# Logits maximum one step later with blanks in the work list; the opening's loads set by hand between the first transposing DMAs

## The chip, the core and the metric

The kernel runs on one core of a Trainium2 chip. The core has TensorE (PE: matrix products, written to PSUM), VectorE (DVE), ScalarE (ACT), GpSimd (POOL) and SyncE (SP), which here only issues DMAs; 16 DMA engines move the data. Each engine runs its own instructions in order and waits on semaphores for others. The metric is the device time of one execution in microseconds, lower is better.

## The reference

Attention over 8 batches of 8 heads, 576 positions, 64 wide, with a mask by blocks of 64; then a soft mixture of experts on the 4608 tokens of width 512 (8 experts with 4 slots each, so 32 slots), then a two-layer network. Cut to what matters:

```python
scores = scale * np.matmul(q, k.transpose(0, 1, 3, 2))
scores = np.where(mask, scores, -1000000000.0)        # mask: block_i >= block_j
scores = scores - np.max(scores, axis=-1, keepdims=True)
attn = np.exp(scores)
attn = attn / (np.sum(attn, axis=-1, keepdims=True) + 1e-09)
x = np.matmul(attn, v)                    # -> tokens x of shape (4608, 512)
logits = x @ phi                          # (4608, 32)
d = np.exp(logits - logits.max(0, keepdims=True))
d /= d.sum(0, keepdims=True) + 1e-09
slot_input = d.T @ x                      # per expert: relu(slot_input @ w1) @ w2
...
c = softmax over the slots;  y = c @ slot_out
h = np.maximum(y @ w_in, 0.0);  out = h * h @ w_out
```

## The kernel before, in words

The attention goes through 32 *pairs*: pair n is heads 2j and 2j+1 of batch n // 4, j = n % 4. `pair(n)` emits, in eight slots, the work of several pairs at once: the scores of pair n (`scores`, matmuls L572, L581, L590; ScalarE's exponentials `p` L610, and `pd` L592 for the last diagonal blocks; GpSimd's sums `ss` L615), the products with the values of pair n-1 (`pv`, L646 `xm`, L657 `tl`, L666 `sm`), the row maxima of pair n+2 (`maxpass`, matmuls L494, L502, L530; VectorE's `pm` and `ptl` L508, and L543 to L552 at its end, which write them into `qb`), and the splitting of pair n+3 into a high and a low half-precision part (`split`: ScalarE L451, VectorE L457; the key tile `ka` is then turned by a transposing DMA L464 into `s`, the high query is turned on TensorE L473).

Ahead of a split stands `scale`: ScalarE squares the keys and the queries (L389, tile `junk`, the sums in `ssq`), TensorE adds them over the partitions (L396, `ps_ssq`), and VectorE makes the factors (L401 to L421). `turn_qb(n)` turns the low query of pair n, with the maxima in it, by a transposing DMA into `t` (L483); it needs L552 of that pair. `s2copy` copies half of `s` from SBUF to SBUF (L980).

Around the pairs runs other work, popped from lists slot by slot: `aux` (the steps of `scale`; `None` is an empty slot), `dq` (SyncE's loads, two a slot: keys and queries of a batch L365 and L371 as well as L343 and L350, values L319 and L324, `phi` L332, weights), and `work`, the list that `batch(b)` makes for the soft mixture of the batch before: `logits(u)` for five blocks of tokens (GpSimd ends them, L762, in `lg` and `ltl`), `maxes` (VectorE L812, L813, and the copy `mx` L815: the maximum of the logits over the tokens of a batch), `running` (the maximum so far, L820), `weights` (the exponentials `d`, L831 to L840), `total` (L880), `tokens(u)` (TensorE L857 turns the attention's output, VectorE L867 multiplies it by the reciprocal of the softmax's sums into `x`), and `gather(u)` (TensorE L906 and L912, VectorE L919: `acc`). A batch's list is put in at the second pair of the next batch, and slots 1, 3, 4, 6 and 7 pop one item each, so five a pair.

The order of each engine's instructions is worked out by a scheduler from the program's order, estimated durations and dependences, except where `tc.manual_schedule(engines=...)` keeps the program's order for the engines it names. Before the change the opening (pairs 0 to 2 scaled, split and maximised ahead of the pair loop) keeps it for ScalarE alone; the pair loop keeps it for TensorE and SyncE. `order(x, y)` makes x come after y.

Of the kernel before, what the change touches and what calls it, by code (L numbers as in the profile page):

```python
# [13 lines left out]
ALU = mybir.AluOpType  # L14
AX = mybir.AxisListType
# [8 lines left out]
def tile_attn_soft_moe_ffn(  # L24
# [225 lines left out]
    def attention():  # L250
# [481 lines left out]
        def batch(b):  # L732
# [77 lines left out]
            def maxes():  # L810
                mxb = sm_p.tile([128, NSL], F32, tag="mxb", name="mxb")
                nc.vector.tensor_reduce(out=mxb, in_=lm.rearrange("p u s -> p s u"), axis=AX.X, op=ALU.max)  # L812
                nc.vector.tensor_tensor(out=mxb[0:64], in0=mxb[0:64], in1=ltl, op=ALU.max)  # L813
                mx4 = sm_p.tile([128, 4, NSL], F32, tag="mx4", name="mx4", bufs=1)
                nc.vector.tensor_copy(mx4, mxb.unsqueeze(1).to_broadcast([128, 4, NSL]))  # L815
                box["mx4"] = mx4
# [33 lines left out]
            def tokens(u, j0=0, j1=NJ):  # L850
# [9 lines left out]
                if j0 == NJ - 1:  # L860
# [5 lines left out]
                    return  # L866
                nc.vector.tensor_tensor(  # L867
                    out=box[u][0:w].rearrange("p (hp j d) -> p j hp d", hp=2, j=NJ)[:, j0:j1],
# [57 lines left out]
            if b == B - 1:  # L926
# [10 lines left out]
                [lambda u=u: logits(u) for u in range(5)]  # L937
                + [lambda: tokens(0), maxes, lambda: tokens(1), running, lambda: tokens(2), weights, lambda: tokens(3)]
                + [total, lambda: [gather(u) for u in range(4)], lambda: tokens(4), lambda: gather(4)]
            )  # L940
# [35 lines left out]
        def loads(k):  # L976
            for _ in range(min(k, len(dq))):
                dq.pop(0)()
# [3 lines left out]
        prepare()  # L982
        with tc.manual_schedule(engines={mybir.EngineType.Activation}):
            c0, c1, c2 = [scale([i]) for i in range(3)]
            for f in c0[:2] + c1[:1] + c0[2:]:
                f()
            sp0 = split(0)
            for f in (sp0[2], sp0[0], c1[1], c1[2], sp0[1], sp0[3]):
                f()
            sp1 = split(1)  # L990
            for f in (sp1[2], sp1[0], c2[0], c2[1], sp1[1], sp1[3], c2[2]):
                f()
            sp2 = split(2)
            sp2[2]()
            s2copy(0)
            m0 = maxpass(0)
            for f in m0[6:] + m0[:6] + [sp2[0], sp2[1], sp2[3]]:
                f()
        dq += load_v(0) + load_batch(1)[0] + load_batch(1)[1] + load_v(1) + [lambda hp=hp: load_phi(hp) for hp in range(2)]
        s3 = scale([AHEAD])  # L1000
        m1 = maxpass(1)
        for i, f in enumerate(m1[6:] + m1[:6]):
            if i >= 6 and s3:
                [g() for g in s3]
                s3 = []
            f()
            loads(1)
        for f in s3:
# [13 lines left out]
        def pair(n):  # L1022
# [43 lines left out]
            if n >= 7:  # L1066
                if ew:
                    dq.append(ew.pop(0))
                if len(decq) <= 6 and nraw[0] < NRAW:
                    nraw[0] += 1  # L1070
                    decq.append(nraw[0] - 1)
            if n == 1:
                aux += scale([4]) + scale([5])
            if n == 2:
                aux += scale([6])
            if n % 2 and n > 1:
# [28 lines left out]
            for i in range(8):  # L1105
                loads(2)
                for f in slot.get(i, []):
                    f()
                f = aux.pop(0) if aux else None
                if f:  # L1110
                    f()
                elif decq and i % 8:
                    dec_step()
                for _ in range((i in (1, 3, 4, 6, 7)) if n < N - 3 else 1 if n < N - 1 else 2):
                    if work:
                        work.pop(0)()
            if n == N - AHEAD - 1:
# [645 lines left out]
```

## Time and profile before

| | us |
|---|---|
| median of three runs | 875.07 |
| lowest and highest run | 869.28 and 875.86 |
| the profiled execution | 874.78 |
| its span, first to last instruction | 873.0 |
| TensorE busy in it | 816.3 (94%) |
| VectorE, ScalarE, GpSimd busy | 669.5, 627.8, 242.6 |

The profile is of one execution. It has a page (busy times, the span in 40 slices, the chain of waits that ended last, groups of instructions), and the trace behind it can be asked for timelines, lists of waits, and windows. A time in a timeline is counted from the span's start. "Wait" is the idle time of an engine ahead of an instruction, put down to what ended it.

### The profile page before, as it was taken

What the parts mean: (1) busy time and instruction counts of PE and PEld (TensorE: products, weight loads), DVE (VectorE), ACT (ScalarE), POOL (GpSimd) and SP (SyncE); (2) the same over time, 40 slices, a digit from 0 to 9 for tenths busy, and PEclk for the clock granted to TensorE, in tenths of its full rate; (3) what the DMA queues carried; (4) which work ended last, traced back from release to release, by engine and by line L of the source; (5) the groups of instructions that cost most, each with busy time, mean ns of one, the idle gap of its engine ahead of it and who ended that gap; (6) DMA issues with size and microseconds to landing.
All of it is one profiled execution on the core that took longest, in us unless ns stands there. A gap on an engine that the chain in (4) does not pass through costs nothing.

```text
span 873.0 us, 21653 instructions
## 1 busy us (share of the span) xinstructions
PE 816.3 (94%) x8741; PEld 598.9 (69%) x8741; DVE 669.5 (77%) x1546; ACT 627.8 (72%) x996; POOL 242.6 (28%) x394
## 2 busy tenths in 40 slices
PE   2779999899999999999995999999999999999997
PEld 1446767576666667676431554888888888888887
DVE  5857789989998987764724899787888888888880
ACT  5579787777878687744214889888888888888770
POOL 0245747556575757464000000000000000000000
PEclk9899999999999999999999899999999999999999
DMA  8798998999899978689999300101000000000002
GB/s 166 148 188 159 156 200 155 219 172 221 156 210 181 171 149 171 119 232 314 351 386 385 123 1 0 50 26 45 30 25 26 25 26 25 26 25 26 26 25 49
DMA packets 220356, 113.14 MB, mean 130 GB/s; under 512 B 192096, under 2 KB 194144, under 8 KB 220256
## 3 DMA queue, kind: packets, MB, share of 16 engines
q1 hardware_dynamic: 217600, 111.11, 55.1%
q8 instruction: 68, 1.11, 0.6%
q10 hardware_dynamic: 2656, 0.66, 0.4%
q14 instruction: 32, 0.26, 0.1%
HBM read 78.71 MB, written 9.44 MB: 101 GB/s over the span
## 4 chain that ended last, share of the span: by engine, by line
PE 71%; DMA 9%; DVE 6%; POOL 5%; ACT 4%; issue 2%; SPq 1%; ACTq 0%; POOLq 0%
PE ps_y L1575 14%; PE ps_z L1575 10%; PE ps_x L1575 10%; PE xm L646 7%; PE ps_sc L572 6%; DMA t<-qb 4%; PE ps_hb L1539 3%; DMA wch<-in_moe_w_dram 3%; POOL ul L762 2%; PE ps_max L494 2%; PE sm L666 2%; POOL ss L615 2%; PE po L1597 2%; PE ps_u L753 2%; PE tl L657 2%
## 5 line engine op out<-in xcount | busy, mean ns | idle before, releaser
L1575 PEld LDWEIGHTS <-ah 128*128 128x128 f16 x1792 | 174.8, 98 | 21.9 <-issue 0.8
L610 ACT ACTIVATE p<-ps_sc,es 128x512 f32<-128x512 f32 x192 | 130.1, 686 | 64.7 <-PE ps_sc L572 32.5
L1507 DVE TENSOR_TENSOR al<-a,ah 128x1024 f16<-128x1024 f32 (+1 forms) x128 | 138.5, 1124 | 16.9 <-ACT ah L1562 15.5
L508 DVE TENSOR_REDUCE pm<-ps_max 128x4 f32<-128x512 f32 x160 | 106.1, 681 | 39.5 <-PE ps_max L502 39.3
L615 POOL TENSOR_TENSOR ss<-p 128x384 f32<-128x384 f32 (+1 forms) x128 | 86.3, 693 | 156.3 <-ACT p L610 156.1
L1562 ACT CAST ah<-a 128x1024 f16<-128x1024 f32 (+1 forms) x128 | 114.4, 936 | 15.0 <-DVE a L1507 13.4
L572 PE MATMUL ps_sc<-t,s 128*128 128x512 f16 (+3 forms) x512 | 108.4, 305 | 12.7 <-DMA t<-qb 7.6
L1668 POOL TENSOR_TENSOR ot<-u,p 128x256 f32<-128x256 f32 x16 | 12.5, 781 | 374.2 <-DVE u L1639 358.5
L1575 PE MATMUL ps_y<-bh,al 128*128 128x256 f16 x384 | 104.6, 273 | 0.0
L1575 PE MATMUL ps_y<-bl,ah 128*128 128x256 f16 x384 | 104.6, 272 | 0.0
L1575 PE MATMUL ps_y<-bh,ah 128*128 128x256 f16 x384 | 104.6, 272 | 0.0
L615 POOL TENSOR_TENSOR ss<-ss,p 128x320 f32<-128x320 f32 (+1 forms) x128 | 98.3, 768 | 18.7 <-ACT p L610 11.1
L1575 PEld LDWEIGHTS <-al 128*128 128x128 f16 x896 | 87.6, 98 | 10.2
L1401 ACT ACTIVATE r<-ps_hb,cts_h 128x1024 f32<-128x1024 f32 x64 | 71.2, 1112 | 30.0 <-PE ps_hb L1539 29.4
L646 PE MATMUL xm<-p,ar_hi 128*64 128x256 f32 (+3 forms) x512 | 87.2, 440 | 0.0
L1507 DVE TENSOR_TENSOR a<-a 128x256 f32<-128x256 f32 x192 | 76.1, 424 | 3.9
L1575 PE MATMUL ps_x<-bh,ah 128*128 128x256 f16 x256 | 69.8, 273 | 0.0
L1575 PE MATMUL ps_z<-bh,ah 128*128 128x256 f16 x256 | 69.8, 273 | 0.0
L1575 PE MATMUL ps_x<-bl,ah 128*128 128x256 f16 x256 | 69.8, 273 | 0.0
L1575 PE MATMUL ps_z<-bh,al 128*128 128x256 f16 x256 | 69.8, 273 | 0.0
L1575 PE MATMUL ps_x<-bh,al 128*128 128x256 f16 x256 | 69.8, 273 | 0.0
L1575 PE MATMUL ps_z<-bl,ah 128*128 128x256 f16 x256 | 69.8, 273 | 0.0
(272 smaller groups left out, 1777.9 us busy)
## 6 DMA issues: line engine op xcount, KB each, us to landing
wch<-in_moe_w_dram SPq DMA_DIRECT2D x18, 1024.0 KB, 12.8
ar_hi<-in_v_dram SPq DMA_DIRECT2D x64, 128.0 KB, 3.9
raw<-in_moe_w_in_dram SPq DMA_DIRECT2D x16, 512.0 KB, 5.7
out_dram<-ot SPq DMA_DIRECT2D x32, 256.0 KB, 2.1
ar_hi<-in_moe_w_dram SPq DMA_DIRECT2D x6, 1024.0 KB, 8.3
s<-s SPq DMA_DIRECT2D x32, 144.0 KB, 3.7
ar_hi<-in_k_dram SPq DMA_DIRECT2D x16, 256.0 KB, 4.5
ar_hi<-in_q_dram SPq DMA_DIRECT2D x16, 256.0 KB, 4.7
```

The source lines that it names most:

```text
L494: nc.tensor.matmul(ps[:, c0:c0 + 128 * (u + 1)].rearrange("p (s c) -> p s c", c=128), t1[:, 2 * u + hp, :], s1[:, hp:2 * u + 2:2, :], star ...
L508: nc.vector.tensor_reduce(out=o, in_=i, axis=AX.X, op=ALU.max)
L572: nc.tensor.matmul(ps[:, c0:c0 + w].rearrange("p (s c) -> p s c", c=128), kk[:, 2 * t + hp, :], qq[:, 2 * u0 + hp:8:2, :], start=(c0 == 0 ...
L610: exps[:] = [nc.scalar.activation(out=pt, in_=ps, func=AF.Exp, scale=es[:, 0:1])]
L615: add = lambda o, x, y: nc.gpsimd.tensor_tensor(out=o, in0=x, in1=y, op=ALU.add)
L646: nc.tensor.matmul(box["xm"][64 * hp:64 * hp + 64, 128 * t:512], vs[:, t, hp, :], r, start=(t == 0), stop=(t == 3),)
L657: nc.tensor.matmul(box["tl"][64 * hp:64 * hp + 64, 0:64], vs[:, t, hp, :] if t < NU else v_tail(b)[:, j, :], r, start=(t == 0), stop=(t == ...
L1401: nc.scalar.activation(out=r[:, c0:c1], in_=ps[:, c0:c1], func=AF.Relu, **kw)
L1507: sub = lambda o, a, b: nc.vector.tensor_tensor(out=o, in0=a, in1=b, op=ALU.subtract)
L1539: nc.tensor.matmul(ps[:, 512 * j + 256 * a:512 * j + 256 * a + 256], w[:, 128 * f:128 * f + 128], c, start=True, stop=True,)
L1562: nc.scalar.copy(v(hl[n % 2][0][:, 2 * kq:2 * kq + 2], s), v(a7[n, kq], s))
L1575: nc.tensor.matmul(acc[:, 0:HM], a[:, k], b[:, k], start=bool(first and k + j == 0), stop=(k == KH - 1 and j == 2), skip_group_check=not f ...
```

## The change

Three edits. In `batch(b)` the list gets the order `tokens(0), tokens(1), maxes, tokens(2), running, tokens(3), None, weights, None, total, gathers, tokens(4), gather(4)`, so `maxes` comes one item later, there are two empty items, and all from `running` on come one to three items later; the reduction of `maxes` is tied behind the last token multiply on VectorE, but in the last batch. In the opening SyncE's order is the program's too, `dq` begins with the keys and queries of batch 1 and has the values of batch 0 behind them, and `loads` is called between the splits. And `scale` for pairs 4, 5 and 6 is put in one pair earlier each (pairs 0, 1 and 2; in pair 0 behind four empty slots), each alone and with an empty slot between squares and factors.

```diff
--- before.py
+++ after.py
@@ -809,7 +809,9 @@
 
             def maxes():
                 mxb = sm_p.tile([128, NSL], F32, tag="mxb", name="mxb")
-                nc.vector.tensor_reduce(out=mxb, in_=lm.rearrange("p u s -> p s u"), axis=AX.X, op=ALU.max)
+                x = nc.vector.tensor_reduce(out=mxb, in_=lm.rearrange("p u s -> p s u"), axis=AX.X, op=ALU.max)
+                if b < B - 1:
+                    order(x, box["x"])
                 nc.vector.tensor_tensor(out=mxb[0:64], in0=mxb[0:64], in1=ltl, op=ALU.max)
                 mx4 = sm_p.tile([128, 4, NSL], F32, tag="mx4", name="mx4", bufs=1)
                 nc.vector.tensor_copy(mx4, mxb.unsqueeze(1).to_broadcast([128, 4, NSL]))
@@ -864,7 +866,7 @@
                             func=AF.Copy, scale=rc[0:w, u, 2 * j0 + hp:2 * j0 + hp + 1],
                         )
                     return
-                nc.vector.tensor_tensor(
+                box["x"] = nc.vector.tensor_tensor(
                     out=box[u][0:w].rearrange("p (hp j d) -> p j hp d", hp=2, j=NJ)[:, j0:j1],
                     in0=pt[0:w, 0:128 * nj].rearrange("p (j hp d) -> p j hp d", hp=2, j=nj),
                     in1=rc[0:w, u, 2 * j0:2 * j1].rearrange("p (j hp) -> p j hp", hp=2).unsqueeze(3).to_broadcast(
@@ -935,8 +937,9 @@
                 )
             return (
                 [lambda u=u: logits(u) for u in range(5)]
-                + [lambda: tokens(0), maxes, lambda: tokens(1), running, lambda: tokens(2), weights, lambda: tokens(3)]
-                + [total, lambda: [gather(u) for u in range(4)], lambda: tokens(4), lambda: gather(4)]
+                + [lambda: tokens(0), lambda: tokens(1), maxes, lambda: tokens(2), running]
+                + [lambda: tokens(3), None, weights, None, total]
+                + [lambda: [gather(u) for u in range(4)], lambda: tokens(4), lambda: gather(4)]
             )
 
         def recycle():
@@ -980,31 +983,42 @@
         s2copy = lambda n: nc.sync.dma_start(out=s2[n % NB2][0:64], in_=T[n][1][0:64])
         loads(len(dq))
         prepare()
-        with tc.manual_schedule(engines={mybir.EngineType.Activation}):
+        dq += load_batch(1)[0] + load_batch(1)[1] + load_v(0) + load_v(1) + [lambda hp=hp: load_phi(hp) for hp in range(2)]
+        s3 = scale([AHEAD])
+        E = mybir.EngineType
+
+        def opening():
             c0, c1, c2 = [scale([i]) for i in range(3)]
             for f in c0[:2] + c1[:1] + c0[2:]:
                 f()
             sp0 = split(0)
             for f in (sp0[2], sp0[0], c1[1], c1[2], sp0[1], sp0[3]):
                 f()
+            loads(3)
             sp1 = split(1)
             for f in (sp1[2], sp1[0], c2[0], c2[1], sp1[1], sp1[3], c2[2]):
                 f()
+            s2copy(0)
+            loads(2)
             sp2 = split(2)
             sp2[2]()
-            s2copy(0)
+            loads(3)
             m0 = maxpass(0)
             for f in m0[6:] + m0[:6] + [sp2[0], sp2[1], sp2[3]]:
                 f()
-        dq += load_v(0) + load_batch(1)[0] + load_batch(1)[1] + load_v(1) + [lambda hp=hp: load_phi(hp) for hp in range(2)]
-        s3 = scale([AHEAD])
-        m1 = maxpass(1)
-        for i, f in enumerate(m1[6:] + m1[:6]):
-            if i >= 6 and s3:
-                [g() for g in s3]
-                s3 = []
-            f()
-            loads(1)
+
+        with tc.manual_schedule(engines={E.SP}):
+            with tc.manual_schedule(engines={E.Activation, E.SP}):
+                opening()
+            m1 = maxpass(1)
+            for i, f in enumerate(m1[6:] + m1[:6]):
+                if i >= 6 and s3:
+                    [g() for g in s3]
+                    s3 = []
+                if i in (2, 5):
+                    loads(1)
+                f()
+            loads(2)
         for f in s3:
             f()
         work, aux, decq, nraw = [], [], [], [0, 0]
@@ -1069,10 +1083,8 @@
                 if len(decq) <= 6 and nraw[0] < NRAW:
                     nraw[0] += 1
                     decq.append(nraw[0] - 1)
-            if n == 1:
-                aux += scale([4]) + scale([5])
-            if n == 2:
-                aux += scale([6])
+            if n < 3:
+                aux += [None] * (0 if n else 4) + scale([n + 4], 1)
             if n % 2 and n > 1:
                 ns = [i for i in (n + AHEAD + 1, n + AHEAD + 2) if i < N]
                 aux += scale(ns, 2) if ns else []
@@ -1112,8 +1124,9 @@
                 elif decq and i % 8:
                     dec_step()
                 for _ in range((i in (1, 3, 4, 6, 7)) if n < N - 3 else 1 if n < N - 1 else 2):
-                    if work:
-                        work.pop(0)()
+                    f = work.pop(0) if work else None
+                    if f:
+                        f()
             if n == N - AHEAD - 1:
                 dq += wchunks(2)
             if n == N - 1:
```

The code lines behind L812 move by 2 and behind L983 by 3 and more, so that `x` is L869, the copy `mx` L817 and `s2copy` L983 in the changed kernel. The numbers behind a tile's name count tiles and differ for the same tile.

SyncE in the opening, before, from the first turned key tile (`s_248`, pair 0) to the fourth (`s_476`, pair 3); `t_381` and `t_467` are the turned queries of pairs 0 and 1:

```order
L371 DMA ar_hi<-in_k_dram 64x4x64
L980 DMA s_0_144<-s_248 64x1152
L371 DMA ar_hi<-in_k_dram 64x4x64
L464 DMA_TRANSPOSE s_293<-ka 128x9x128
L365 DMA ar_hi<-in_k_dram 128x8x64
L980 DMA s_1_145<-s_293 64x1152
L365 DMA ar_hi<-in_k_dram 128x8x64
L464 DMA_TRANSPOSE s_339<-ka 128x9x128
L365 DMA ar_hi<-in_k_dram 128x8x64
L483 DMA_TRANSPOSE t_381<-qb_141 128x9x128
L483 DMA_TRANSPOSE t_467<-qb_142 128x9x128
L464 DMA_TRANSPOSE s_476<-ka 128x9x128
```

The same place after (`s_299` is the key tile of pair 1, `s_485` of pair 3, `t_392` and `t_473` the queries):

```order
L365 DMA ar_hi<-in_k_dram 128x8x64 x2
L983 DMA s_1_145<-s_299 64x1152
L464 DMA_TRANSPOSE s_348<-ka 128x9x128
L365 DMA ar_hi<-in_k_dram 128x8x64
L371 DMA ar_hi<-in_q_dram 64x4x64 x2
L319 DMA ar_hi<-in_v_dram 128x4x64
L483 DMA_TRANSPOSE t_392<-qb_141 128x9x128
L365 DMA ar_hi<-in_q_dram 128x8x64 x2
L483 DMA_TRANSPOSE t_473<-qb_142 128x9x128
L365 DMA ar_hi<-in_q_dram 128x8x64 x2
L324 DMA ar_hi<-in_v_dram 64x4x64
L464 DMA_TRANSPOSE s_485<-ka 128x9x128
```

The keys' loads of batch 1 stand ahead of the queries' transposes, its queries' loads around them, and the loads of the values (L319, L324), which were ahead of the first key transpose, stand behind.

TensorE at the end of the scores of pair 0 (L590), before:

```order
L590 LDWEIGHTS s_248
L590 MATMUL ps_sc<-t_247,s_248 128x128
L590 LDWEIGHTS s_0_144
L590 MATMUL ps_sc<-t_381,s_0_144 128x128
L572 LDWEIGHTS s_293
L572 MATMUL ps_sc<-t_292,s_293 128x512
```

And after:

```order
L590 LDWEIGHTS s_251
L590 MATMUL ps_sc<-t_250,s_251 128x128
L590 LDWEIGHTS s_0_144
L590 MATMUL ps_sc<-t_392,s_0_144 128x128
L396 MATMUL ps_ssq<-ssq,ones 128x2
L572 LDWEIGHTS s_299
L572 MATMUL ps_sc<-t_298,s_299 128x512
```

The norm of pair 4 (L396), which before stood in the middle of pair 1 behind the second part of its maxima, now stands ahead of the first score of pair 1.

ScalarE there, before, from the exponentials of pair 0 on:

```order
L610 ACTIVATE p<-ps_sc,es 128x512 x5
L592 ACTIVATE pd<-ps_sc,es 128x128
L610 ACTIVATE p<-ps_sc,es 128x512
L389 ACTIVATE junk,ssq<-ar_hi 128x576
L695 COPY xt<-xm 128x512
L698 COPY xt<-tl 128x64
L610 ACTIVATE p<-ps_sc,es 128x512 x2
L389 ACTIVATE junk,ssq<-ar_hi 128x576
```

And after:

```order
L610 ACTIVATE p<-ps_sc,es 128x512 x4
L389 ACTIVATE junk,ssq<-ar_hi 128x576
L610 ACTIVATE p<-ps_sc,es 128x512
L592 ACTIVATE pd<-ps_sc,es 128x128
L389 ACTIVATE junk,ssq<-ar_hi 128x576
L610 ACTIVATE p<-ps_sc,es 128x512
L389 ACTIVATE junk,ssq<-ar_hi 128x576
L451 ACTIVATE qa<-ar_hi,sig 128x576
```

The squares of pair 4 (the first two of L389) stand ahead of the first exponential of pair 1; those of pair 5 begin behind it.

VectorE in the second pair that holds the list of batch 0, around `maxes`, after (before, L812 stood ahead of the first `x` of the list, in the row ahead of L421):

```order
L869 TENSOR_TENSOR x<-ps_x,rc 128x4x2x64
L508 TENSOR_REDUCE pm_146<-ps_max 128x4
L508 TENSOR_REDUCE pm_146<-ps_max 128x2x2
L869 TENSOR_TENSOR x<-ps_x,rc 128x4x2x64
L508 TENSOR_REDUCE pm_146<-ps_max 128x4
L812 TENSOR_REDUCE mxb<-lg 128x32
L508 TENSOR_REDUCE pm_146<-ps_max 128x4
L815 TENSOR_TENSOR mxb<-mxb,ltl 64x32
L869 TENSOR_TENSOR x<-ps_x,rc 128x4x2x64
L817 COPY mx_1855<-mxb 128x128
L543 TENSOR_REDUCE ps_max<-pm_146 128x2x2
L457 SCALAR_TENSOR_TENSOR qb_142<-ar_lo,sig,qa 128x9x64
```

The reduction, the maximum with the tail and the copy stand behind the second and third `x` now.

VectorE in the first pair of the batch after, up to the L552 that releases a turned query, after (before, the multiply of 64 partitions stood behind the L552 of the pair ahead, and an `acc` in this stretch ahead of the reciprocals):

```order
L719 RECIPROCAL rc<-ps_sT 128x2x8 x2
L723 RECIPROCAL rc<-ps_sT 64x8
L869 TENSOR_TENSOR x<-ps_x,rc 64x4x2x64
L508 TENSOR_REDUCE pm_146<-ps_max 128x4
L196 SCALAR_TENSOR_TENSOR tin<-dec_sq,raw 128x512
L921 SCALAR_TENSOR_TENSOR acc<-acc,al,ps_dx 128x512
L508 TENSOR_REDUCE pm_146<-ps_max 128x4
L202 TENSOR_SCALAR dec_sq<-tin 128x512
L543 TENSOR_REDUCE ps_max<-pm_146 128x2x2
L208 SCALAR_TENSOR_TENSOR dec_sq<-tin,dec_sq 128x512
L544 TENSOR_REDUCE ps_max<-pm_146 128x2x2
L457 SCALAR_TENSOR_TENSOR ka<-ar_hi,sig,ka 128x9x64
```

The multiply of the fifth block of tokens (`x`, 64 partitions) and an `acc` of a gather stand in this stretch, ahead of its L552, which is four rows on.

## Rows read from the trace of the kernel before

**Rows 1.** Head of the page; granted clock of TensorE in 40 slices.

```profile
span 873.0 us, 21653 instructions
...
PEclk9899999999999999999999899999999999999999
```

**Rows 2.** TensorE's timeline, opening: start, duration, line, operation; [idle before, what ended it].

```profile
32.94 0.58 PE L572 MATMUL ps_sc<-t,s 128*128 128x512 f16 x1 [2.93 <-DMA t<-qb]
...
40.65 0.28 PE L590 MATMUL ps_sc<-t,s 128*128 128x128 f16 x2
...
48.30 0.38 PE L396 MATMUL ps_ssq<-ssq,ones 128*128 128x2 f32 x2 [1.25 <-ACT junk L389]
...
49.93 0.38 PE L572 MATMUL ps_sc<-t,s 128*128 128x256 f16 x2
...
53.15 0.38 PE L396 MATMUL ps_ssq<-ssq,ones 128*128 128x2 f32 x2 [2.36 <-ACT junk L389]
...
61.56 0.39 PE L494 MATMUL ps_max<-s,t 128*128 128x128 f16 x2 [2.01 <-DMA s<-ka]
...
63.06 0.53 PE L396 MATMUL ps_ssq<-ssq,ones 128*128 128x2 f32 x2
...
66.15 0.40 PE L572 MATMUL ps_sc<-t,s 128*128 128x256 f16 x1
```

**Rows 3.** TensorE's waits, 100 to 420 us: total, times, longest.

```profile
PE ps_sc L572 <- DVE pm L508: 4.8, 4, 1.8
PE ps_sc L572 <- DMA t<-qb: 4.7, 5, 1.9
```

**Rows 4.** Windows of the opening: length, TensorE busy, granted clock, DMA share, GB/s.

```profile
33.00:39.00 6.00, 6.00 (x46) 0.50 0.57 109
53.00:55.00 2.00, 1.85 (x26) 1.00 1.10 241
63.00:66.00 3.00, 3.00 (x16) 0.50 1.15 219
```

**Rows 5.** SyncE's timeline (SPq: DMA issues; duration is that of issuing).

```profile
39.11 3.23 SPq L365 DMA_DIRECT2D ar_hi<-in_q_dram  x4
...
188.35 1.31 SPq L483 DMA_TRANSPOSE t<-qb  x1
...
237.07 1.31 SPq L483 DMA_TRANSPOSE t<-qb  x1
```

**Rows 6.** TensorE's timeline, start of a pair in the loop.

```profile
221.32 0.38 PE L572 MATMUL ps_sc<-t,s 128*128 128x512 f16 x1 [0.62 <-DMA t<-qb]
```

**Rows 7.** Windows of the loop, all engines' busy time, clock, DMA share, GB/s.

```profile
196.00:231.00 35.00, 32.39 (x465) 21.27 (x463) 32.01 (x86) 27.45 (x54) 20.16 (x32) 1.00 1.18 224
231.00:237.00 6.00, 6.00 (x104) 4.03 (x104) 6.00 (x13) 5.10 (x12) 3.18 (x5) 1.00 0.20 57
```

**Rows 8.** ScalarE's timeline, opening.

```profile
39.13 2.16 ACT L610 ACTIVATE p<-ps_sc,es 128x512 f32<-128x512 f32 x3 [0.70 <-PE ps_sc L572]
41.19 0.36 ACT L592 ACTIVATE pd<-ps_sc,es 128x128 f32<-128x128 f32 x1
...
47.48 0.67 ACT L389 ACTIVATE junk<-ar_hi 128x576 fp8e4<-128x576 f32 x1
```

**Rows 9.** Chain of waits, opening: start, duration up to the landing.

```profile
29.70 3.19 DMA t<-qb
...
56.86 4.65 DMA s<-ka
```

**Rows 10.** TensorE's waits, 285 to 420 us, the longest two.

```profile
PE ps_sc L572 <- DVE pm L508: 1.8, 1, 1.8
PE ps_dx L912 <- DVE x L867: 0.8, 1, 0.8
```

**Rows 11.** Instructions of L867 and L815: count, shortest/median/longest ns, when, shapes.

```profile
L867 DVE TENSOR_TENSOR x<-ps_x,rc x41: 273/673/692, 107.0 to 415.3; 128x512 f32<-128x512 f32 x28, 64x512 f32<-64x512 f32 x7, 128x256 f32<-128x256 f32 x3, 128x128 f32<-128x128 f32 x3
...
L815 DVE COPY mx<-mxb x8: 208/226/1349, 105.6 to 418.0; 128x128 f32<-128x128 f32 x8
```

## The prediction

> **What bounds the kernel now.** I read the head of the page first [rows 1]: the span is 873.0 us, and the profiled execution took 874.78 us, so 1.8 us lie outside the span; the median of the three runs is 875.07 us. TensorE's granted clock is below nine tenths in two slices of forty only, so what can be won is idle TensorE and a few stretches at the half clock. Next the timeline of TensorE in the opening [rows 2], for rows that end with a wait: 1.25 us at 48.30 and 2.36 us at 53.15 for ScalarE's squares (`junk`), ahead of the norms of pairs 4 and 5; 2.93 us at 32.94 for the first turned query tile, and 2.01 us at 61.56 for the turned key tile `s` of pair 4. Then the list of what TensorE waits for from 100 to 420 us [rows 3]: four waits for VectorE's `pm` reductions, 4.8 us together, and five for turned query tiles, 4.7 us.
>
> The clock is the third view [rows 4]. After the 2.93 us wait TensorE runs at 1.2 GHz from 33 to 39 us; after the 2.01 us wait it does so from 63 to 66 us. After the wait at 53.15 the clock stays at 2.4 GHz. The second dip has a price in the timeline [rows 2]: from the norm matmul to the 128x256 score of the same pair takes 48.30 to 49.93 = 1.63 us in pair 1 and 63.06 to 66.15 = 3.09 us in pair 2, so 1.46 us.
>
> Last, the loop. SyncE sits idle until VectorE ends the maximum of a pair (L552) and then issues a turned tile; this "restart" comes at 188.35 and at 237.07 [rows 5]. TensorE gets the first turned query tile of the next batch at 221.32, 32.97 us behind the restart [rows 6], and the DMA engines are queued more than full in that stretch (1.18), but at 0.20 in the 6 us before a restart [rows 7]. From 221.32 to the next restart TensorE's pace rules: 15.75 us. So a cycle of four pairs is a DMA part and a TensorE part. What is saved ahead of the transfer's landing inside the DMA part is given back as a longer wait for that transfer.
>
> **The opening.** The change takes the squares of pair 4 into pair 0, those of pair 5 into pair 1, and loads batch 1's keys and queries between the first transposing DMAs, when SyncE was idle.
> Removed: the waits at 48.30 and 53.15, 1.25 + 2.36 = 3.61 us, since both norms no longer stand behind those squares.
> Added: on TensorE the norm of pair 4 now stands between the last score of pair 0 (L590, ends at 40.65 + 0.28 = 40.93) and the first of pair 1, and in ScalarE's order the second square comes behind four exponentials, the first square, the fifth exponential and `pd`. From ScalarE's timeline [rows 8]: exponentials step by 2.16/3 = 0.69, so the fourth ends at about 40.5. The first square takes 0.67, the fifth exponential 0.69, `pd` 0.36 (each overlaps its neighbour by up to 0.1), and from a square's start to its norm matmul it is 48.30 − 47.48 = 0.82. So 40.5 + 0.67 + 0.69 + 0.36 + 0.82 = 43.0, less 0.2 for the overlaps, and TensorE waits 42.8 − 40.9 = 1.9 us where it did not. Bounds: 1.2 if the first square fits into ScalarE's idle time of 0.70 ahead of the row, 2.6 if a square waits for its load by one more square. I take 1.9. Behind that waiting instruction stand the score of pair 1 and all of `pv(0)`; nobody else waits for them, since ScalarE has the squares to do.
> The `s` of pair 4: SyncE issues it at 56.86 right behind a row of loads without a gap, and it lands 4.65 us later [rows 9]. After the change five loads fewer lie between the fourth key transpose and this one; a row of four loads takes 3.23 us on SyncE [rows 5], 0.8 each, and I take 0.65 for five of which two are short: 3.2 us. So it is issued at 53.6 and lands at 56.8 to 58.3 (3.19 us on idle queues, 4.65 on full ones). TensorE comes there at 59.55 − 3.61 + 1.9 = 57.8. So 0 to 0.5 of the 2.01 us stays; I take 0.5, as the queues are full. Then the half-clock stretch behind it goes as well: −1.46.
> At nothing: the values of batch 0's first pair are loaded later, now around the query transposes (29.70 on, [rows 9]) and behind the fourth key transpose; `pv(0)` reads them behind 43 us, and the wait for the square covers it. Without that cover it would wait for one load's landing at most, 3 to 5 us. The other moved loads stand ahead of where they were.
> One more term has only bounds. Loads of a key, of two query tails and of values, 0.5 MB, now stand right ahead of the first query transpose at 29.70, for which TensorE waits 2.93 us. It landed in 3.19 us on idle queues; the key transpose on full ones took 4.65 [rows 9]. So 0 to +1.46. At 241 GB/s [rows 4] 0.5 MB is 2.1 us, and SyncE was idle ahead of 29.70, so they have gone through by then: I take 0, nearest to the idle row. The Trainium skill speaks against that choice: DMA: Bandwidth & Descriptors, Latency and other measured facts, says that the fixed cost of a transfer grows with the load on HBM. The 3.19 against 4.65 here agrees. By the rule the first transpose would land later by part of the 1.46, and the sum would be up to 871.8.
> Opening: −3.61 + 1.9 − 1.5 − 1.46 = −4.7 us.
>
> **The loop.** `maxes` stands behind the second `tokens` step now, so GpSimd has one step more to finish the logits. VectorE's waits for it at L812 go, and with them those of TensorE for `pm`, which comes behind L812 on VectorE: 4.8 us. Three of the four lie in the DMA parts of cycles and come back as waits for `t<-qb`: gain 0. From 285 us on there is one of 1.8 us, and the next longest of all is for another thing [rows 10]: no turned tile is late there, so this one is won: −1.8.
> Against it: the work list is longer by two blanks, so `tokens(4)` lands in the next batch's first pair, whose `pm` pass ends in the L552 that restarts SyncE. VectorE is without a gap in 231 to 237 (6.00 of 6.00 us, [rows 7]), so the 0.67 us of L867 [rows 11] move the restart by that much. It counts in the three cycles that DMA limits: +2.0. In the pair of the fourth restart TensorE does not wait.
> `running`, `weights`, `total` and the gathers come one or two slots later; they write only what the next batch reads, so nothing waits within a pair; at the end of attention the weights' transfers, which follow TensorE, carry a shift through. I cost these at 0, ±0.3.
> Loop: −1.8 + 2.0 = +0.2.
>
> **Sum.** 874.78 − 4.7 + 0.2 = 870.3 by the profiled execution; by the median 0.3 more. I say 870.
>
> **The rivals.**
> (a) The loop does not give back. For it: every cycle also has TensorE's part, and SyncE waits for TensorE and VectorE inside the DMA part too, so an earlier TensorE may bring later issues forward. Against it: the 32.97 us and the queue at 1.18. Then all 4.8 us are won and the 2.0 are not lost: 874.78 − 4.7 − 4.8 = 865.3; faster by over 1%.
> (b) Slower: the four first pairs pay. The copy of the maxima (L815) took 1.349 us in its longest case against a median of 0.226 [rows 11], while GpSimd was at work on the sums. If the token multiply in its new place were stretched so, each of four restarts slips by 0.67 + 1.12 = 1.8 us, 7.2 together, and the 1.8 at `pm` is not won: 874.78 − 4.7 + 7.2 = 877.3. It decides from 1.2 us a restart on (4.7/4). Against it: the multiply has run beside GpSimd 41 times between 0.273 and 0.692 us, never longer [rows 11]. By the Trainium skill (SBUF — State Buffer, Who interferes with whom) a VectorE instruction with one input from SBUF, as this one (the other is in PSUM), does not contend with GpSimd, and a copy may; the rows agree for both. By it this rival is left with 0.67 a restart, 2.7 in all, and is not slower.
> (c) The new wait of 1.9 us at 41 brings a half-clock stretch of its own, as 2.01 did at 61.56, while 1.25 and 2.36 did not. Price 1.46 (or 3.0, half of 33 to 39): 871.8 to 873.3.
> (d) The opening does not do what it says, since the first query transpose or `s` of pair 4 is late by as much as it won: +1.46 + 1.5 + 1.46 on my sum: 874.7.
>
> **How the numbers follow.** Forecast (870) 0.43; (a) 0.19; (c) 0.20; (d) 0.12; (b) 0.06. About 1% (8.75 us) is what a measurement of this kernel can tell from no change: the three runs alone lie between 869.28 and 875.86. From 870 down to (a), with half a microsecond for its terms, 864.5; up past (d), 876. That leaves out most of (b) and the far side of (a). Faster by over 1% (below 866.3): (a) and a little of the forecast, 0.20. Slower by over 1% (above 883.8): only (b) with more than it is priced at, 0.02. Within: 0.78. The forecast's own range is 868.5 to 872.
>
> **What would show it.** In the changed profile: no wait at the norms of pair 1, a wait of 1.2 to 2.6 us for `junk` near 41 us; the `s` of pair 4 issued near 53.6 and a wait of at most 0.5 behind it; full clock from 60 to 68 us; no wait of VectorE at L812; in the loop the waits for `pm` gone but those for `t<-qb` longer by the same; restarts 0.7 us later behind the first scores of a batch. Wrong would be: waits for `t<-qb` that stay as short as they are (then a), the clock at half near 43 (c), a landing of the first query transpose past 33.5 (d).

## The result, and the profile after

The changed kernel takes 884.23 us (883.76 to 886.77), the kernel before 873.15 us in the runs beside it: a ratio of 1.0149, 95% interval 1.0116 to 1.0181. It is slower by 13.0 us at the middle of that interval, where 870 was forecast. The profiled execution took 884.6 us with a span of 882.8, so 9.8 us more than the profile before. One run of the old list below, which took 947.23 us at a mean granted clock of 0.846, is left out of its time and ratio.

The head of the page of the changed kernel, with the granted clock in 40 slices and the engines' shares of the chain that ended last, and those shares before:

```profile
span 882.8 us, 21649 instructions
...
PEclk9899999999999999999998899999999999999999
...
PE 68%; DVE 15%; DMA 8%; ACT 4%; issue 3%; SPq 1%; ACTq 0%; DVEq 0%
```

```profile
PE 71%; DMA 9%; DVE 6%; POOL 5%; ACT 4%; issue 2%; SPq 1%; ACTq 0%; POOLq 0%
```

VectorE's share of the chain is 15% in place of 6%. To find where that comes from, I cut the program in two at the last score of pair 3 (L590), which is ahead of all list work. TensorE's timeline there, first before, then after:

```profile
75.79 0.28 PE L590 MATMUL ps_sc<-t,s 128*128 128x128 f16 x2
```

```profile
70.12 0.28 PE L590 MATMUL ps_sc<-t,s 128*128 128x128 f16 x2
```

So the opening gives 5.7 us, and the rest of the program loses 9.8 + 5.7 = 15.5. A second cut, at the transpose of the last batch's maxima (L820 at 418.41 before, L822 at 427.05 after), splits that. Windows between the two cuts, before and then after (length, TensorE busy, granted clock, DMA share, GB/s):

```profile
75.79:418.41 342.62, 330.07 (x4573) 1.00 0.94 188
70.12:427.05 356.93, 333.35 (x4573) 0.99 0.93 182
```

So 14.3 of the 15.5 us are lost between the cuts: TensorE is idle for 23.6 us in place of 12.6, and busy for 3.3 us more. The other 1.2 us come behind the second cut and were not traced. TensorE's timeline of the changed kernel's opening, which answers to [rows 2]:

```profile
33.25 0.59 PE L572 MATMUL ps_sc<-t,s 128*128 128x512 f16 x1 [3.66 <-DMA t<-qb]
...
42.58 0.38 PE L396 MATMUL ps_ssq<-ssq,ones 128*128 128x2 f32 x2 [1.89 <-ACT junk L389]
```

The waits at 48.30, 53.15 and 61.56 are gone. One of 1.89 us has come at the norm of pair 4, and the wait for the first query transpose is 0.73 us longer. The loop is another picture. The whole list of what TensorE waits for from 100 to 420 us, which answers to [rows 3]:

```profile
PE ps_mx L822 <- DVE mx L817: 9.5, 6, 1.7
PE ps_ds L882 <- ACT d L842: 7.7, 7, 1.7
PE ps_dx L914 <- DVE x L869: 4.0, 7, 0.8
PE ps_sc L572 <- DMA t<-qb: 0.9, 1, 0.9
PE ps_x L859 <- ACT p L610: 0.5, 1, 0.5
```

That is 22.6 us. Before, the list came to 12.2: the 9.5 in [rows 3] and four small waits (1.1 for `p` at the norms, 0.8 and 0.4 at the gathers, 0.4 for `mx`). None of the first three was a steady wait before; the 4.8 us for `pm` are gone and the 4.7 for `t<-qb` are 0.9. They are the transpose of the maxima in `running`, the column sums in `total`, and `gather(4)`. The first place, on TensorE and then on VectorE:

```profile
103.45 0.28 PE L590 MATMUL ps_sc<-t,s 128*128 128x128 f16 x2
103.56 0.61 PE L859 MATMUL ps_x<-ident,xt 128*128 128x128 f32 x4
105.89 0.33 PE L822 MATMUL ps_mx<-ident,mx 128*128 128x128 f32 x1 [1.72 <-DVE mx L817]
106.05 0.59 PE L572 MATMUL ps_sc<-t,s 128*128 128x512 f16 x2
```

```profile
104.07 0.68 DVE L508 TENSOR_REDUCE pm<-ps_max 128x4 f32<-128x512 f32 x1
104.67 0.19 DVE L815 TENSOR_TENSOR mxb<-mxb,ltl 64x32 f32<-64x32 f32 x1
104.78 0.67 DVE L869 TENSOR_TENSOR x<-ps_x,rc 128x512 f32<-128x512 f32 x1
105.39 0.45 DVE L817 COPY mx<-mxb 128x128 f32<-128x128 f32 x1
```

TensorE turns the third block of tokens and then stands at the transpose of `mx` (L822). VectorE still has to end a `pm` reduction and the multiply of that block, and only then copies the maxima. The next pair's scores, which start at once when L822 has run, stand behind it in TensorE's queue. The second place, on TensorE and then on ScalarE:

```profile
164.76 0.28 PE L590 MATMUL ps_sc<-t,s 128*128 128x128 f16 x2
164.87 0.38 PE L396 MATMUL ps_ssq<-ssq,ones 128*128 128x4 f32 x2
166.97 0.39 PE L882 MATMUL ps_ds<-ones,d 128*32 128x1 f32 x10 [1.72 <-ACT d L842]
...
168.62 0.58 PE L572 MATMUL ps_sc<-t,s 128*128 128x512 f16 x1 [0.94 <-DMA t<-qb]
```

```profile
164.71 1.26 ACT L610 ACTIVATE p<-ps_sc,es 128x512 f32<-128x512 f32 x2
165.94 0.66 ACT L193 ACTIVATE dec_sq<-raw 128x512 f32<-128x512 f32 x1
166.50 0.21 ACT L841 ACTIVATE d<-d 64x32 f32<-64x32 f32 x1
166.62 0.29 ACT L842 ACTIVATE d<-d 128x128 f32<-128x128 f32 x1
```

ScalarE makes `d` behind two exponentials and a step of the weights' decoding, and TensorE waits for it. Last, windows of the opening behind the `s` of pair 4, of the place of `mx`, of the second place, and of its like in the next two batches, which answer to [rows 4]:

```profile
60.00:68.00 8.00, 8.00 (x133) 1.00 1.06 201
103.00:107.00 4.00, 2.28 (x21) 1.00 1.31 240
166.00:173.00 7.00, 5.09 (x48) 0.76 1.17 245
217.00:224.00 7.00, 5.22 (x42) 0.76 1.32 231
268.00:275.00 7.00, 5.94 (x56) 0.76 1.35 224
```

The half-clock stretch of the opening at 63 us is gone, as forecast. Three new ones stand in the loop, each behind `total`, and 0.24 of 7 us in each is 1.7 us. The timeline gives nearly the same price: from the start of L882 to that of the L473 behind it TensorE takes 5.39 us at 218.95 and 5.29 at 269.78, but 3.65 at 320.46, where the clock stayed at 2.4 GHz.

### The profile page after: what moved, and what is told of

Same layout as the page of the kernel before. It is cut to its first block, busy times and chain, and to the rows that moved or that the text cites. A ratio compares the mean times of both kernels' runs of the same rounds, so it can differ in the third digit from the quotient of the medians.

```text
span 882.8 us, 21649 instructions
## 1 busy us (share of the span) xinstructions
PE 817.9 (93%) x8741; PEld 598.3 (68%) x8741; DVE 670.7 (76%) x1546; ACT 625.6 (71%) x996; POOL 250.8 (28%) x394
## 4 chain that ended last, share of the span: by engine, by line
PE 68%; DVE 15%; DMA 8%; ACT 4%; issue 3%; SPq 1%; ACTq 0%; DVEq 0%
PE ps_y L1588 14%; PE ps_z L1588 10%; PE ps_x L1588 10%; PE xm L646 7%; PE ps_sc L572 5%; DVE pm L508 3%; PE ps_hb L1552 3%; PE ps_u L753 3%; DMA t<-qb 3%; DMA wch<-in_moe_w_dram 3%; PE po L1610 2%; PE sm L666 2%; PE ps_max L494 2%; PE tl L657 2%; PE ps_h L1234 2%
## 5 line engine op out<-in xcount | busy, mean ns | idle before, releaser
L615 POOL TENSOR_TENSOR ss<-p 128x384 f32<-128x384 f32 (+1 forms) x128 | 91.8, 736 | 155.2 <-ACT p L610 155.1
L646 PE MATMUL xm<-p,ar_hi 128*64 128x256 f32 (+3 forms) x512 | 90.7, 454 | 0.0
```

Of the source, the lines that this page charges most:

```text
L615: add = lambda o, x, y: nc.gpsimd.tensor_tensor(out=o, in0=x, in1=y, op=ALU.add)
L646: nc.tensor.matmul(box["xm"][64 * hp:64 * hp + 64, 128 * t:512], vs[:, t, hp, :], r, start=(t == 0), stop=(t == 3),)
```

## The experiments

Theory 1, formed from these rows, is that the loss is TensorE's in-order queue. The new list puts three steps right behind what they need, and everything behind them waits. (Counted in the two lists, `running` comes one item later, `weights`, `total`, the gathers and the fifth tokens step two, and the second to fourth tokens steps one earlier; "one to three items later" above is not exact.) Its rivals are theory 2, that the new opening puts the loop into a worse rhythm; theory 3, the one that the prediction priced, that the fifth token multiply ahead of L552 delays SyncE; and theory 4, that the tie itself costs, wherever the steps stand. A ratio is always to the kernel before on the same chip.

**The old list in the new opening.**

```diff
-                if b < B - 1:
-                    order(x, box["x"])
...
-                + [lambda: tokens(0), lambda: tokens(1), maxes, lambda: tokens(2), running]
-                + [lambda: tokens(3), None, weights, None, total]
...
+                + [lambda: tokens(0), maxes, lambda: tokens(1), running, lambda: tokens(2), weights, lambda: tokens(3)]
+                + [total, lambda: [gather(u) for u in range(4)], lambda: tokens(4), lambda: gather(4)]
```

> The changed kernel with the work list of before and without the tie of the maximum; the new opening stays. Theory 1 (neighbours: in the new list three steps of TensorE per batch, the transpose for the running maximum, the column sums of total, and the last gather, stand right behind what they need, and TensorE waits there 1.6, 1.2 and 0.6 us in each of seven batches; the opening's gain of 5.6 us carries through): 866 to 870 us. Theory 2 (the new opening puts the loop's loads and turned tiles into a worse rhythm, and that is the loss): 880 us or more. Theory 3 (the fifth token multiply ahead of the maxima's end delays SyncE): 866 to 870 as in theory 1.

Measured: 868.47 us, ratio 0.996 (0.9934 to 0.9985). Theory 2 falls: the opening by itself gains. A second set of runs of the same kernel, beside later ones:

> The list of before without the tie in the new opening, once more beside the two others: 868.5, so a ratio of 0.996 to the kernel before.

Measured: 867.4 us, ratio 0.9941 (0.9917 to 0.9966). At the middle of these two intervals the opening is worth 3.5 and 5.1 us.

**The new list in the old opening.** The opening and the line `if n < 3: aux += ...` as before, list and tie as changed.

> The changed kernel with the opening and the places of the scale steps of before; new list and tie stay. Theory 1: the loop's loss alone, 884.2 + 5.6 = 889.8, so 887 to 892 us, with the waits for mx, d and x in the loop. Theory 2: about 873. Theory 3: 887 to 892, but no more than small waits at the three places.

Measured: 890.48 us, ratio 1.0219 (1.0184 to 1.0254). The list costs 19 us by the kernel before, and the two halves add up: 1.0219 less 0.004 to 0.006 is near 1.0149. TensorE's waits are the same three, 9.7 us for `mx`, 7.6 for `d` and 4.0 for `x`; this profile has half-clock stretches behind five of the waits for `d`, two more than the changed kernel's.

**The tie taken away.** The two lines `if b < B - 1: order(x, box["x"])` left out of the changed kernel.

> The changed kernel without the tie of the maximum's reduction behind the token multiply (the scheduler then puts it where it was, ahead of the first token multiply); list with blanks and opening stay. Theory 1: the wait for mx goes (7 x 1.6 = 11.5 us), those for d and x stay, and TensorE's waits for pm (up to 4.8 us) come back: 874 to 878 us. Theory 3: 884, since the fifth token multiply stays where it is. Theory 2: 884.

Measured: 880.34 us, ratio 1.0103 (1.0062 to 1.0145), 2.3 us beyond what theory 1 gave. The list of waits says why:

```profile
PE ps_ds L880 <- ACT d L840: 5.4, 7, 1.2
PE ps_sc L572 <- DMA t<-qb: 5.2, 3, 2.9
PE ps_dx L912 <- DVE x L867: 4.0, 7, 0.8
PE ps_max L494 <- DVE pm L508: 3.6, 4, 0.9
```

The waits for `mx` went, but those for turned tiles came up from 0.9 to 5.2 us. What I had expected to be won was in part given back to the DMAs.

**The steps set apart with blanks.**

```diff
-                + [lambda: tokens(0), lambda: tokens(1), maxes, lambda: tokens(2), running]
-                + [lambda: tokens(3), None, weights, None, total]
+                + [lambda: tokens(0), lambda: tokens(1), maxes, lambda: tokens(2), None]
+                + [running, lambda: tokens(3), weights, None, None, total]
```

> The changed kernel with the blanks placed otherwise: one between the third tokens step and running, running then ahead of the fourth tokens step, two blanks between weights and total, so total, the gathers, tokens(4) and gather(4) fall into the next batch's first pair with scores and maxima in between. Theory 1: all three waits go, and what stays is the opening's gain and the pm waits won where DMA does not limit: 864 to 869 us. Theory 3: about 884, since the fifth token multiply still stands ahead of the maxima's end in that pair. Theory 2: 884.

Measured: 872.40 us, ratio 1.0008 (0.9986 to 1.003). Twelve of the changed kernel's 13 us are gone, which theory 3 and theory 2 don't allow; but the time is above theory 1's range too, and some 4 us above the old list's. All three waits are down to 1.7 us together, and others stand in their place:

```profile
PE ps_sc L572 <- DMA t<-qb: 9.6, 5, 4.0
PE ps_nb L833 <- DVE nm L827: 2.7, 6, 0.5
PE ps_dx L914 <- DVE x L869: 1.0, 4, 0.3
PE ps_mx L822 <- DVE mx L817: 0.4, 1, 0.4
```

At two of the waits for turned tiles the clock fell as well: it is 0.51 from 165 to 172 us and 0.66 from 219 to 224 us, a loss of 5.1 us. Why the turned tiles are late here was not tried.

**The tie alone, and the swap alone.** Both in the new opening: the old list with the tie, and the old list with `maxes` and `tokens(1)` changed over and the tie. The second one's line, cut short:

```diff
-                + [lambda: tokens(0), maxes, lambda: tokens(1), running, ...
+                + [lambda: tokens(0), lambda: tokens(1), maxes, running, ...
```

> The list of before with the tie alone (the maximum's reduction behind the first token multiply of the list), in the new opening. Theory 1 (neighbours): the running maximum's transpose keeps scores and another tokens step between itself and the copy of the maxima, so no wait for mx of over 0.5 us; VectorE's waits for GpSimd and TensorE's for pm go, three of four pm waits come back as waits for t<-qb: 866 to 869 us. Theory 4 (the tie itself, a later maximum, is what costs, wherever the steps stand): waits for mx of 1 us and more a batch, 875 to 880.

> The list of before with maxes and the second tokens step changed over and the tie, no blanks, nothing else later; new opening. The transpose for the running maximum then has one stretch of scores between itself and the copy of the maxima. Theory 1: a wait for mx of 0 to 0.7 us a batch, none for d and x, pm waits gone: 866 to 870. Theory 4: 875 to 880.

Measured: 870.12 us, ratio 0.9981 (0.9962 to 0.9999) for the tie, 886.81, ratio 1.0171 (1.0144 to 1.0198) for the swap. My bound for the wait of `mx` failed in both, and by far in the second. The time of the tie lies between the ranges of the two theories, that of the swap above both. In the list of waits of the tie alone:

```profile
PE ps_mx L822 <- DVE mx L817: 8.8, 7, 1.8
```

And of the swap, TensorE's wait in its timeline, and VectorE's timeline at that place:

```profile
157.51 0.30 PE L822 MATMUL ps_mx<-ident,mx 128*128 128x128 f32 x1 [3.89 <-DVE ps_max L543]
```

```profile
154.22 1.09 DVE L196 SCALAR_TENSOR_TENSOR tin<-dec_sq,raw 128x512 f32<-128x512 f32 x1 [0.57 <-ACT dec_sq L193]
155.23 0.36 DVE L812 TENSOR_REDUCE mxb<-lg 128x32 f32<-128x128 f32 x1
155.51 0.67 DVE L508 TENSOR_REDUCE pm<-ps_max 128x4 f32<-128x512 f32 x1
156.11 0.35 DVE L815 TENSOR_TENSOR mxb<-mxb,ltl 64x32 f32<-64x32 f32 x1
156.39 0.41 DVE L202 TENSOR_SCALAR dec_sq<-tin 128x512 uint32<-128x512 uint32 x1
156.72 0.64 DVE L817 COPY mx<-mxb 128x128 f32<-128x128 f32 x1
157.29 0.16 DVE L543 TENSOR_REDUCE ps_max<-pm 128x4 f32<-128x16 f32 x1
```

With the tie the scheduler sets the maxima among steps of the decoding and of the row maxima, and TensorE waits 3.9 us. The profile names L543 as what ended the wait; the copy, which the transpose reads, ended 0.09 us earlier, and so I count these waits as waits for `mx`. The tie with its waits of 8.8 us costs little (2 to 3.5 us beside the ratios of the old list), since the 4.8 us of waits for `pm` go and those for turned tiles are 2.5; the swap has 19.3 us in six waits for `mx`, with half-clock stretches behind five of them, and is 15 us slower than the kernel before. So theory 4 is right for the wait and wrong for both times, and theory 1 has to be put more sharply: what counts is the distance on VectorE as much as that on TensorE, and of 8.8 us of waits most take the place of those that TensorE has for `pm` or turned tiles anyway.

**Weights one item earlier.** `[tokens(3), weights, None, None, total]` in the changed kernel.

> The changed kernel with weights one item earlier (the two blanks both behind it), so that a further stretch of scores and maxima stands between weights and total; all else as changed. Theory 1: TensorE's waits for d (7.7 us) go, and with them the half-clock stretches that follow them at 168, 219 and 270 us; those for mx and x stay; some comes back as waits for t<-qb: 873 to 879. Theory 3 (the fifth token multiply in the next batch's first pair is what costs): 883 to 885.

Measured: 880.06 us, ratio 1.0092 (1.0059 to 1.0125), just beyond the top of theory 1's range. The waits for `d` fell to 3.8 us, not to nothing, and `t<-qb` took 2.6. Of the half clock 3.4 us are left in place of 5.0, in one stretch (0.57 from 167 to 175 us) around a wait of 2.1 us for a turned tile.

**The fifth token step late, alone.** The old list in the new opening with `None, None` ahead of `tokens(4)` and a `None` behind it.

> The list of before without the tie, in the new opening, with two blanks ahead of the fifth tokens step and one ahead of its gather, so that the fifth token multiply and the gather's accumulation stand in the next batch's first pair as in the changed kernel, ahead of the maxima's end there, but with scores between them on TensorE. Theory 3 (they delay SyncE's next turned tile by 0.7 to 2 us in each of the three or four cycles that DMA limits): 2 to 6 us over the list of before in the same opening, 870.5 to 875, with longer waits for t<-qb. Theory 1 alone: no change, 868 to 870.

Measured: 868.61 us, ratio 0.9945 (0.9922 to 0.9967), the same as the old list beside it. In its profile the multiply stands ahead of the L552 as it should (174.54 and 181.38), and SyncE's restarts are 48.3 and 47.0 us apart, in the old list 49.2 and 47.4. Theory 3 falls, and with it a term of my sum.

**The changed list with none of the three neighbours.**

```diff
-                if b < B - 1:
-                    order(x, box["x"])
...
-                + [lambda: tokens(3), None, weights, None, total]
+                + [lambda: tokens(3), weights, None, None, None, total]
```

> The changed kernel without the tie, with weights one item earlier and three blanks between weights and total, so total, the gathers, tokens(4) and gather(4) stand in the next batch's first pair with scores and maxima between them: the changed list, its token steps and blanks kept, but with none of the three neighbours. Theory 1 (the waits at the three neighbours, and the half-clock stretches behind them, are the whole loss): the time of the list of before in the same opening, a ratio of 0.994 to 0.998 (867 to 871 us), no wait of over 0.5 us for mx, d or x. If something else of the new list costs (the later steps keep SyncE's turned tiles waiting for VectorE): 872 to 880, with waits for t<-qb of 4 us and more.

Measured: 870.82 us, ratio 0.9995 (0.9967 to 1.0023). The time is in theory 1's range, the ratio just past it. Of the waits, `mx` and `d` have one each, of 0.4 and 0.6 us, and `x` five of 1.3 us together. The whole isn't won back: 4.8 us of waits for turned tiles and 3.7 at L494 stand in this profile, and the clock is 0.57 from 115 to 123 us, around one of the former, a loss of 3.4 us. By these ratios the tie and the three neighbours are 13 of the 17 to 18 us between the old and the new list (1.0149 − 0.9995 of 1.0149 − 0.996, or of 1.0149 − 0.9941). The rest, 3 to 5 us, is left to the later steps of the list. It is little more than the intervals allow, and which step makes the turned tiles late was not tried.

**The two halves of the opening.** First the loads without the earlier scale steps (the old list; `if n == 1: aux += scale([4]) + scale([5])`, `if n == 2: aux += scale([6])`), then the earlier scale steps alone in the kernel before.

> The list of before without the tie, the new SyncE order in the opening, but the scale steps of pairs 4 to 6 where they were (pairs 1 and 2). It tells which half of the opening gains its 5.6 us. If the earlier scale steps: the waits for junk at the norms of pairs 4 and 5 come back, less what an earlier load saves, and s of pair 4 stays late: 870 to 873 us by the median, span about 872. If the loads: span near 867, as with both.

> The kernel before with the scale steps of pairs 4 to 6 one pair earlier alone; old list, old order of SyncE's loads. The squares of pair 4 then wait on ScalarE for queries whose loads are issued at 39 to 42 us and land near 46, and the norm and all scores of pair 1 wait behind them. If the loads are what makes the earlier scale steps possible: a wait of 4 us and more at that norm, and a time of 873 to 878; if the scale steps gain by themselves: 867 to 869.

Measured: 870.02 us, ratio 0.9988 (0.9966 to 1.0011), and 875.62, ratio 1.003 (1.001 to 1.0049). The second has the wait that was expected, on TensorE and in the chain:

```profile
47.60 0.59 PE L396 MATMUL ps_ssq<-ssq,ones 128*128 128x2 f32 x2 [8.47 <-ACT junk L389]
```

```profile
41.25 4.94 DMA ar_hi<-in_q_dram
```

The scale steps need the loads: without them ScalarE stands at a square until the query has landed at 46.2, and TensorE for 8.47 us. The loads alone are not told from no change by the ratio. The start of the last score of pair 3, where the opening was read above, tells the halves apart better: 75.79 and 75.05 us with neither (the kernel before and the new list in the old opening), 73.50 with the loads alone, 77.62 with the steps alone, and 69.35 to 70.78 with both, in ten profiles. So the loads give some 2 us there by themselves, the steps lose some 2 without the loads, and on top of them they gain 3 to 4. Both together gain 0.4 to 0.6% of the time.

## Why the prediction was wrong

**The opening: right.** Forecast −4.7 us, measured −5.7 in the profile at pair 3 and 3.5 to 5.1 by the ratios of the old list in it. The wait at the moved norm was put at 1.9 and came out at 1.89. (The step of 0.69 in that sum is (41.19 − 39.13)/3; 2.16/3, as written there, is 0.72.) The `s` of pair 4 was forecast to be issued at 53.6 and was issued at 52.29:

```profile
52.29 1.40 SPq L464 DMA_TRANSPOSE s<-ka  x1
```

No wait is left behind it, where I kept 0.5. The first query transpose was put at 0 of 0 to +1.46; its landing took 3.91 us instead of 3.19 [rows 9], so half of the bound:

```profile
29.30 3.91 DMA t<-qb
```

The rule of the Trainium skill that the prediction set against its own choice (DMA: Bandwidth & Descriptors, Latency and other measured facts: more load, a larger fixed cost) agrees with this row better than the choice did; it speaks of HBM, and this transfer goes from SBUF to SBUF. In the nine other profiles with this opening the wait is 3.06 to 3.43 us, so it grew by 0.1 to 0.7 us, and the changed kernel's profile has the most. The other page named there (SBUF — State Buffer, Who interferes with whom) agrees too: the token multiply took at most 0.692 us in its new places, and rival (b), which needed 1.8, did not come. Added up from the rows, the terms as they came out are −0.4 ahead of the first query transpose (TensorE begins to wait for it at 29.59 in place of 30.01), +0.7 at it, −3.6 and +1.9 at the norms, −2.0 at the `s` of pair 4 and −1.5 of half clock: −4.9, and 0.8 of the 5.7 I can't place.

**The loop: the step that failed** is the one sentence "`running`, `weights`, `total` and the gathers come one or two slots later; they write only what the next batch reads, so nothing waits within a pair", costed at 0, ±0.3. It asked who reads what these steps write, and not whom they wait for themselves and what stands behind them. Three of them sit in TensorE's queue, ahead of the next scores, and each now came close behind its producer on another engine: 9.5 + 7.7 + 4.0 = 21.2 us of waits. By the whole lists that is 22.6 us in place of 12.2, so 10.4 more, and by the windows TensorE's idle time grew by 11.0. The three half-clock stretches took some 5.0 more. That is 16, where 14.3 were lost between the cuts: TensorE's busy time grew by 3.3 only, so 1.7 of other busy time went the other way, which I can't place. The prediction also had no term for what the tie costs, with which the waits for `mx` come to 8.8 us in the old list too, and without which they go in the new one. The change as printed showed the place: `tokens(2), running` stand side by side in the list, and among VectorE's rows the copy `mx` stands right behind the third `x`. The prediction did not read those rows for what waits. It gave 0.02 to a time above 883.8, by rival (b) alone, and 884.23 was measured.

**The fifth multiply ahead of L552, +2.0:** 0 by its own experiment. The late multiply did not move SyncE's restarts further apart. The waits for turned tiles also differ between two profiles of one kernel, the old list in the new opening (3.8 and 1.2 us); that the DMAs do not hold a cycle at 33 us is likely from both, but not shown. It weakens the rule "gain 0" for three of the four `pm` waits as well, which was right only in the looser sense that the tie alone moved the time little.

**The rivals.** None was this one. The slower rival had the right sign and another mechanism; of what it named, a stretched copy of the maxima did occur (0.45 us in the row above against a median of 0.22), but that is a small part of a wait of 1.72 us. Rival (c), a half-clock stretch behind the new wait of 1.9 us, is not in the changed kernel's profile (1.00 from 42 to 47 us), but it is in two of the nine others with this opening (0.66 there).

## What to carry to other kernels

When a step is moved within an in-order queue, cost its inputs before its outputs: who makes what it reads, how many instructions lie between the two on both engines, and what ready work stands behind it. A blank or a swap in a work list moves every later item against the fixed work around it, so each moved step's new neighbours have to be read, not only those the change is about. And moving work ahead pays only together with the loads that feed it: here the steps without their loads lost some 2 us at pair 3, and with them they gained.

## What was not expected of the hardware

The length of a wait did not tell whether a stretch at 1.2 GHz follows. The wait of 1.72 us for `mx` that ends at 105.89 left the clock at 2.4 GHz, while a shorter one in the same profile stands right ahead of the stretch at 270 us:

```profile
269.78 0.36 PE L882 MATMUL ps_ds<-ones,d 128*32 128x1 f32 x9 [1.06 <-ACT d L842]
...
320.46 0.39 PE L882 MATMUL ps_ds<-ones,d 128*32 128x1 f32 x10 [1.08 <-ACT d L842]
```

The wait for the same step at 320.46 is as long and has none behind it. In the old opening the same list, with nearly the same waits, has five such stretches instead of three. In the swapped list five of six waits have such a stretch behind them, the shortest of 2.15 us, and one of 2.14 has none; behind a wait of 3.9 (one window of that kernel):

```profile
158.00:162.00 4.00, 4.00 (x21) 0.58 1.03 211
```

At 0.42 of 4 us that is 1.7 us, nearly half of the wait again. And the wait for `d` of 1.06 us cost more in clock (1.6 us by the timeline) than in idle time. What decides whether the clock falls, these runs don't show.
